# A convolution and a quick-GELU block in fast matrix forms: weight forms summed by ScalarE copies and accumulating transfers, other homes for one step's taps, and one multiply-add moved

## The chip, the core and the metric

The kernel runs on one core of one Trainium2 chip. The metric is device time in microseconds (us) of one execution. The kernel before took 2304.2 us in the median of three runs (2303.05 to 2304.34).

The engines are named as the profile names them: PE (TensorE matrix multiplies, with PEld for its weight loads), ACT (ScalarE), DVE (VectorE), POOL (GpSimd) and SP (SyncE, which here only issues transfers). Each engine works through its own queue in order; a wait at the head of a queue holds everything behind it. Transfers (DMA) are issued from the queues of SP, ACT or POOL.

## The reference

```python
# x: (8, 4096, 192) f32; weight: (8 heads, 7 taps)
w = softmax(weight)                                  # over the 7 taps
conv[b, s, d] = sum_k w[d // 24, k] * x[b, s - 6 + k, d]     # zero before the sequence
h = conv.reshape(32768, 192) @ w_in                  # w_in: (192, 2048)
g = h * sigmoid(1.702 * h)
out = g @ w_out                                      # w_out: (2048, 192)
```

## The kernel before, in words

The tokens are worked in 32 steps ("big", 0 to 31). A step takes 512 tokens of each of two halves of the batch. A step has three stages.

1. **Preparation of the step's input.** `x` is fetched by SP into `xin`, turned by DVE (`transpose_x`), and convolved into `conv_t`. The 192 channels are three blocks c = 0, 1, 2 of 64. Block 1 is summed on DVE: one multiply and six multiply-adds (`conv`, L485). Blocks 0 and 2 go by taps (`tap`): ACT multiplies the shifted input by tap k into a "home" in SBUF (L496). For block 2, POOL then adds home after home to the sum (L498). For block 0 the seven products are summed by a tree of six accumulating transfers issued from POOL's queue (L502, `TREE`), of which the fifth adds home 5 to home 3 and the sixth adds home 3 to the sum. Eight linear combinations of the sums (`sums_c`, POOL; DVE for step 1) give further inputs, and `cross` copies them to the other half of the partitions.
2. **The first product** (`hidden`, called twice per step, v = 0 and v = 1): 21 products (`TERMS`, matmuls at L584) of combined inputs with combined blocks of `w_in`, in a fast matrix form. ACT copies partial results out of PSUM (`copy2`, L621), DVE adds them (`sum2`, L625), ACT applies the GELU (L606 and L610) and writes into the tile `g`.
3. **The second product** (`second`): 25 products (matmuls at L935) of combined blocks of `g` with combined blocks of `w_out`, in an order written out by hand (`PLAN`).

While step n is in its products, step n+1 or n+2 is being prepared. The work of preparation is in two lists. `todo` holds DVE's multiply-adds of block 1 and then POOL's combinations; a call `work(us)` in `hidden` takes items from it while their planned costs (0.48 us for the first multiply, 0.76 us for a multiply-add, nothing for POOL's) fit into its budget, with 0.2 us of tolerance. `ready` holds the taps, which `next_tap` takes one by one.

The homes of the taps lie in the tile `g`, in places whose contents have been used. `spot(i)` for i of 5 and more is one block of `g`. In the steps from 3 on, block 0 uses the spots 13, 16 and 15, and block 2 the spots 14, 17 and 18 (`TAP_SPOTS`). In step 2, block 0 uses six rows of `g` of its own (`first_taps`), which share memory with spots 14, 17 and 18, where block 2 of that step has its homes. The scheduler of the program makes an instruction that overwrites a place wait for all earlier readers of it.

Step 0 is different. Its first product is plain (`plain`), its second product is `second_first`, and meanwhile the weights are rounded on DVE and combined: `w_in` by DVE (`sums_w_in`), `w_out` into the 25 "forms" by POOL (`add_forms`, L387 and L389). Fifteen forms are made at one place in `second_first`, four at its end (`SUMS_O_LATE`). Six are turned in sign later by ACT (`end_forms`, L432). The taps of step 2 are begun in `second_first`: the seven of block 0 there, the seven of block 2 in the first call of `hidden` of step 1. Step 1's `hidden` starts on PE when the last matmuls of `second_first` are done.

In one v = 0 call of `hidden` the order on DVE is: work(2.0), a sum into x, work(1.2), the two sums of k15 and k19, work(1.1), work(2.2), the sums of k20 and k16. For the steps from 2 on that is three items of block 1, then one, then three. The places in the code:

```python
sum2(vec.tensor_sub, x, z, k15)              # L680
work(1.2)                                    # L683, v = 0
sum2(vec.tensor_sub, k15, y, k19)            # L691, waits for ACT's copy k19
sum2(vec.tensor_add, k20, k20, sums)         # L709, ACT's GELU at L711 waits for it
```

Of the kernel before, what the change touches and what calls it, by code (L numbers as in the profile page):

```python
# [11 lines left out]
ALU = mybir.AluOpType  # L12
# [3 lines left out]
def kernel(  # L16
# [29 lines left out]
    nc = tc.nc  # L46

    B, S, D = x.shape
    H, K = weight.shape
# [31 lines left out]
    vec, act = nc.vector, nc.scalar  # L81
# [42 lines left out]
    def row(n, i):  # L124
        return g[:, i // NG, n, :, i % NG, :]
# [13 lines left out]
    def spot(i):  # L139

        if i >= SPOTS:
            return block(*divmod(i - SPOTS, NG))
        flat = osbs[:, i * BLK : (i + 1) * BLK] if i < 2 else room[:, ROOMS[i - 2], :]
        return flat.rearrange("p (k t) -> p k t", k=NG)

    KEPT_LATE, TAP_SPOTS = 3, {0: (13, 16, 15), 2: (14, 17, 18)}

    def kept(i):

# [26 lines left out]
    def own(big):  # L176
        return conv_t[:, big % 2 * 2, :, :]
# [41 lines left out]
    def form(i):  # L219

        if i < WHOLE:
            return w_out_s[:, i // NG, i % NG * NG : (i % NG + 1) * NG, :]
        return w_form[:, i - WHOLE, :, :]

    FORM_OF = [
        6, 4, 5, 2, 3, 0, 8, 9, 10, 11, 12, 13, 14, 15, 16, 24, 23, 17, 18, 19, 20, 7, 21, 22, 1,
    ]
    SUMS_O = [
# [3 lines left out]
    ]  # L232
    SUMS_O_LATE = [
        (23, 1, "+", 0), (24, 1, "+", 3), (1, 14, "+", 22), (7, 0, "-", 21),
    ]
    TURN_O = (9, 11, 17, 20, 7, 21)

# [71 lines left out]
    for c in range(NC):  # L309
        part = sel[:, c, :].rearrange("i (h q) -> i h q", h=2)  # L310
        for sign in (1, -1):
            nc.gpsimd.affine_select(
                out=part,
                in_=part,
# [70 lines left out]
    def add_up(v, dst, a, op, b, eng=vec):  # L385
        if op == "+":
            eng.tensor_add(v(dst), v(a), v(b))  # L387
        elif op == "-":
            eng.tensor_sub(v(dst), v(a), v(b))  # L389
        elif op == "n":  # L390
            vec.scalar_tensor_tensor(
                out=v(dst), in0=v(a), scalar=-1.0, in1=v(b), op0=ALU.mult, op1=ALU.subtract
            )
        else:
            vec.tensor_scalar_mul(v(dst), v(a), -1.0)
# [27 lines left out]
                    )  # L423
        round_piece(NW + i, dsts)

    def add_forms(items):
        for dst, a, op, b in items:
            add_up(form, dst, a, op, b, eng=nc.gpsimd)

    def end_forms():  # L430
        for i in TURN_O:
            act.mul(form(i), form(i), -1.0)  # L432
# [36 lines left out]
    taps = {c: [spot(i)[:, k : k + 2, :] for i in TAP_SPOTS[c] for k in (0, 2)] for c in TAP_SPOTS}  # L469
    first_taps = [row(0, k) for k in (6, 7, 10, 11, 14, 15)]  # L470

    def tap_home(big, c, k):
        return (first_taps if big < 3 and c == 0 else taps[c])[k - 1]

    def conv_src(big, c, k, ns=slice(0, 2)):
        return xts[big][:, c, ns, Q - PAD + k : Q - PAD + k + T]
# [15 lines left out]
    def tap(big, c, k):  # L492

        dst = own(big)[:, 2 * c : 2 * c + 2, :]
        home = tap_home(big, c, k) if k else dst
        act.mul(home, conv_src(big, c, k), cw[:, c, k : k + 1])  # L496
        if k and c not in DMA_TAPS:
            nc.gpsimd.tensor_add(dst, dst, home)  # L498
            return
        homes = [dst] + [tap_home(big, c, i) for i in range(1, K)]  # L500
        for a, b in TREE.get(k, ()):
            nc.gpsimd.dma_start(out=homes[a], in_=homes[b], accum_op=ALU.add)  # L502

    def sums_c(big, i):
        add_up(
# [87 lines left out]
    def terms(big, v, slot, *ts, first=False):  # L593
        for t in ts:
            product1(slot, *TERMS[t], big, v, first)
            first = False
# [35 lines left out]
    def hidden(big, v, x, z, y, sums, work, fetch, last=lambda: None):  # L632

        def pe(slot, *ts, first=False):
            terms(big, v, slot, *ts, first=first)

        def taps_at(n):
            for _ in range(0 if v else n):  # L640
                next_tap()

        def early(i):
            for item in EARLY_G[i] if v else ():
                sum_g(*item)


        if v:
            pe(z, 7, first=True)
            give(True, big)  # L650
        if v:
            pe(sums, 12)
            copy2(k15, sums)
            pe(x, 5, 17)
        else:
            pe(x, 5)
            pe(sums, 12)
            copy2(k15, sums)
            pe(x, 17)
            taps_at(1)  # L660
        gelu(B11, 0, v, x)
        if not v:
            pe(z, 7, first=True)
        pe(sums, 0)
        copy2(k16, sums)
        taps_at(2)
        last()
        def turn_next():
            if big + 2 < N_BIG:
                need(f"done {big + 1}")  # L670
                turn_x(big + 2)

        early(0)
        if not v:
            work(2.0 if big > 1 else 1.6)
        elif big == 1:
            work(3.2)

        pe(y, 6, 14, first=True)
        sum2(vec.tensor_sub, x, z, k15)  # L680
        early(1)
        if not v or big == 1:
            work(1.2)  # L683
        pe(sums, 13)
        copy2(k19, sums)
        pe(x, 2)
        copy2(k18, x)
        taps_at(2)
        pe(z, 11)
        pe(sums, 20, 10)  # L690
        sum2(vec.tensor_sub, k15, y, k19)  # L691
        gelu(B12, 0, v, sums)
        pe(x, 4)
        copy2(k20, x)
        sum2(vec.tensor_sub, k19, z, k19)
        early(2)
        if not v or big == 1:
            work(1.1)
        gelu(B22, 1, v, k19)
        gelu(B22, 0, v, k15)  # L700
        taps_at(2)
        pe(y, 8)
        pe(sums, 1, 9, first=True)
        pe(y, 15)
        if v and big == 1:
            turn_next()
        elif not v:
            work(2.2 if big > 1 else 1.1)
        sum2(vec.tensor_add, k20, k20, sums)  # L709
        sum2(vec.tensor_sub, k16, y, k16)  # L710
        gelu(B11, 1, v, k20)  # L711
        pe(x, 18)
        gelu(B21, 1, v, x)
        early(3)
        fetch()
        if not v:

            copy2(y, z)
        gelu(B21, 0, v, k16)
        if not v:  # L720
            work(1.2)
        if not v and big > 1:
            turn_next()
        pe(sums, 3, 19)
        if not v:
            work(0.7)
        sum2(vec.tensor_add, k18, k18, sums)
        return lambda: gelu(B12, 1, v, k18)
# [4 lines left out]
    def second_first(fetch):  # L733
# [29 lines left out]
        c11, a, c12, c21 = (slots[i][h] for h in range(2) for i in range(2))  # L763
        side = []

        def listed(w, t):
            return [(w[:, v, h, :], t[:, v, :, h * T : (h + 1) * T]) for v in range(2) for h in range(2)]
# [12 lines left out]
        def go(bank, steps, first=True, more=False):  # L780
            for i, (w, t) in enumerate(steps):
                for c in range(NC):
                    nc.tensor.matmul(
                        chunk(bank, c), w[:, chunk_cols(c)], t,
                        start=first and i == 0, stop=not more and i == len(steps) - 1, skip_group_check=True,
                    )
                if side:
                    dst, w, t, start, stop, to = side.pop(0)
                    nc.tensor.matmul(dst, w, t, start=start, stop=stop and to is not False, skip_group_check=True)
                    if to is not False:  # L790
                        act.copy(to, dst)
# [11 lines left out]
        go(a, listed(a11, b11))  # L803
        act.copy(p1, whole(a))
        go(c11, rows11[:8], more=True)
        add_forms(SUMS_O)
        work(1.5)
        sub(b12, b22, b12)  # L808
        sub(s3, a11, a21)
# [1 line left out]
        go(a, listed(s2, t2), first=False)  # L811
        act.copy(whole(c12), whole(a))
        go(c11, rows11[8:], first=False)
        work(5.0)
        add(p1, p1, whole(c11))
        turn(0, 0, blocks(p1), js)
# [2 lines left out]
        add(whole(c21), d21, whole(a))  # L819
        work(4.0)  # L820
        go(c12, listed(s4, b22) + rows12[:cut], first=False)
        fetch()
        go(c21, listed(a22, b21), first=False)
        work(3.0)
# [23 lines left out]
    def chunk(t, c):  # L848
        return t[c * Q : (c + 1) * Q]
# [143 lines left out]
    def work(us):  # L993
        while todo and todo[0][1] <= us + 0.2:
            us -= todo[0][1]
            todo.pop(0)[2]()

    def next_tap():
        if ready:
            ready.pop(0)[2]()  # L1000
            while ready and ready[0][1] == 0:
                ready.pop(0)[2]()
# [39 lines left out]
    def first_step(fetch):  # L1042
# [118 lines left out]
            fetch()  # L1161

        second_first(between)
        add_forms(SUMS_O_LATE)
        load_x(3)
        need("sums")

# [10 lines left out]
    def fetch(big, v, slot):  # L1178

        need(f"first {big}")  # L1180
        terms(big, v, slot, 16, first=True)
# [49 lines left out]
```

## Time and profile before

| what | value |
|---|---|
| median of three runs | 2304.2 us |
| the profiled execution | 2305.07 us, of which its span 2303.4 us |
| PE busy | 2279.2 us (99%) |
| DVE busy | 1963.8 us (85%) |
| ACT busy | 1551.3 us (67%) |
| POOL busy | 861.2 us (37%) |
| granted TensorE clock, mean | 0.997 |

The span is the time from the first to the last instruction of the program; the 1.7 us around it belong to the execution's time. A PE that is called busy is not always at its full rate: matmuls are pipelined, and the profile models their ends. In the timeline a row gives start, length, engine, line, operation, destination and source, count, and in brackets the idle time before it with what ended it. The chain gives start, length and what.

### The profile page before, as it was taken

What the parts mean: (1) busy time and instruction counts of PE and PEld (TensorE: products, weight loads), DVE (VectorE), ACT (ScalarE), POOL (GpSimd) and SP (SyncE); (2) the same over time, 40 slices, a digit from 0 to 9 for tenths busy, and PEclk for the clock granted to TensorE, in tenths of its full rate; (3) what the DMA queues carried; (4) which work ended last, traced back from release to release, by engine and by line L of the source; (5) the groups of instructions that cost most, each with busy time, mean ns of one, the idle gap of its engine ahead of it and who ended that gap; (6) DMA issues with size and microseconds to landing.
All of it is one profiled execution on the core that took longest, in us unless ns stands there. A gap on an engine that the chain in (4) does not pass through costs nothing.

```text
span 2303.4 us, 60981 instructions
## 1 busy us (share of the span) xinstructions
PE 2279.2 (99%) x25238; PEld 1266.0 (55%) x25238; DVE 1963.8 (85%) x2794; ACT 1551.3 (67%) x2942; POOL 861.2 (37%) x824
## 2 busy tenths in 40 slices
PE   9889999999999999999999999999999999999999
PEld 5255655655555555556655555555555555555556
DVE  8878888888888888888888888888888888888877
ACT  7267766677666776666776667776667766677654
POOL 0544433344324444234443244443344432344400
PEclk9989999999999999999999999999999999999999
DMA  8456666665665656666656666566666567564443
GB/s 186 84 109 122 116 125 138 125 125 114 122 136 121 140 115 116 125 133 129 125 114 124 136 123 138 112 115 125 137 128 127 112 122 139 121 137 87 91 97 70
DMA packets 266053, 279.82 MB, mean 121 GB/s; under 512 B 117552, under 2 KB 202928, under 8 KB 265648
## 3 DMA queue, kind: packets, MB, share of 16 engines
q0 software_dynamic: 53472, 144.73, 34.9%
q1 hardware_dynamic: 210656, 130.80, 25.3%
q8 instruction: 199, 3.26, 0.6%
q14 instruction: 78, 0.64, 0.1%
q10 hardware_dynamic: 1648, 0.39, 0.1%
HBM read 53.15 MB, written 25.17 MB: 34 GB/s over the span
## 4 chain that ended last, share of the span: by engine, by line
PE 96%; DVE 2%; DMA 1%; ACT 1%; issue 0%; SPq 0%; POOL 0%; DVEq 0%; ACTq 0%; POOLq 0%
PE slot L584 35%; PE slot L935 33%; PE sums L584 16%; PE sums L935 12%; DVE conv_t L485 1%; DMA g<-g 0%; DMA conv_t<-g 0%; DMA xin<-in_x_dram 0%; DVE g L808 0%; DVE room L800 0%; DVE xt L464 0%; DVE conv_t L389 0%; ACT g L496 0%; DVE room L799 0%; ACT conv_t L1040 0%
## 5 line engine op out<-in xcount | busy, mean ns | idle before, releaser
L584 PE MATMUL slot<-conv_t,w_in_s 64*128 64x512 f32 x3740 | 900.8, 593 | 4.0 <-ACT g L496 2.6
L935 PE MATMUL slot<-g,w_form 128*32 128x256 f32 x7024 | 710.3, 379 | 0.0
L584 PEld LDWEIGHTS slot<-conv_t,w_in_s 64*128 64x128 f32 x3740 | 426.8, 187 | 395.1 <-issue 295.9
L584 PE MATMUL sums<-conv_t,w_in_s 64*128 64x512 f32 x1660 | 444.0, 593 | 10.5 <-ACT room L621 10.2
L389 DVE TENSOR_TENSOR g<-g 128x1024 f32<-128x1024 f32 x372 | 444.3, 1222 | 4.0 <-ACT g L610 0.8
L935 PEld LDWEIGHTS slot<-g,w_form 128*32 128x32 f32 x7024 | 373.7, 110 | 119.6
L610 ACT ACTIVATE g<-room 128x1024 f32<-128x1024 f32 x310 | 324.6, 1073 | 77.4 <-DVE room L625 77.1
L960 ACT COPY room<-slot 32x256 f32<-32x256 f32 x434 | 158.9, 366 | 315.4 <-PE slot L935 313.4
L935 PE MATMUL sums<-g,w_form 128*32 128x256 f32 x2648 | 368.8, 379 | 0.0
L935 PE MATMUL slot<-g,w_out_s 128*32 128x256 f32 x4080 | 318.9, 380 | 0.0
L911 POOL DMA_DIRECT2D g<-g x124 | 106.3, 857 | 514.1 <-DVE g L389 227.8
L584 PEld LDWEIGHTS sums<-conv_t,w_in_s 64*128 64x128 f32 x1660 | 197.8, 187 | 182.7 <-issue 122.5
L498 POOL TENSOR_TENSOR conv_t<-conv_t,g 128x512 f32<-128x512 f32 x180 | 266.6, 1481 | 21.8 <-ACT g L496 5.1
L502 POOL DMA_DIRECT2D g<-g x120 | 104.3, 872 | 439.5 <-PE sums L935 128.7
L496 ACT ACTIVATE g<-xt,cw 128x512 f32<-128x512 f32 x360 | 248.6, 729 | 14.3 <-DMA conv_t<-g 12.0
L621 ACT COPY room<-slot 128x512 f32<-128x512 f32 x434 | 231.4, 601 | 34.9 <-PE slot L584 34.9
L485 DVE SCALAR_TENSOR_TENSOR conv_t<-xt,cw,conv_t 128x512 f32<-128x512 f32 (+1 forms) x210 | 231.0, 1100 | 7.9 <-ACT conv_t L483 3.1
L935 PEld LDWEIGHTS slot<-g,w_out_s 128*32 128x32 f32 x4080 | 164.7, 110 | 131.6 <-ACT g L610 13.6
L606 ACT ACTIVATE g<-slot 128x512 f32<-128x512 f32 x334 | 179.8, 592 | 47.9 <-PE slot L584 29.4
L935 PEld LDWEIGHTS sums<-g,w_form 128*32 128x32 f32 x2648 | 178.1, 110 | 36.6
L389 POOL TENSOR_TENSOR conv_t<-conv_t 128x256 f32<-128x256 f32 x180 | 184.4, 1037 | 9.4
L625 DVE TENSOR_TENSOR room<-slot,room 128x512 f32<-128x512 f32 x248 | 156.1, 680 | 37.2 <-ACT room L621 37.2
(184 smaller groups left out, 2811.4 us busy)
## 6 DMA issues: line engine op xcount, KB each, us to landing
g<-g POOLq DMA_DIRECT2D x124, 512.0 KB, 5.8
xin<-in_x_dram SPq DMA_DIRECT2D x240, 180.0 KB, 4.2
conv_t<-conv_t SPq DMA_DIRECT2D x180, 192.0 KB, 3.2
g<-g POOLq DMA_DIRECT2D x120, 256.0 KB, 3.8
out_dram<-osbs SPq DMA_DIRECT2D x186, 128.0 KB, 4.9
g<-osbs POOLq DMA_DIRECT2D x31, 512.0 KB, 4.5
g<-room POOLq DMA_DIRECT2D x31, 512.0 KB, 5.6
conv_t<-g POOLq DMA_DIRECT2D x60, 256.0 KB, 4.7
```

Source lines behind the costliest of these rows:

```text
L389: eng.tensor_sub(v(dst), v(a), v(b))
L485: vec.scalar_tensor_tensor(out=dst, in0=src, scalar=tap, in1=dst, op0=ALU.mult, op1=ALU.add)
L496: act.mul(home, conv_src(big, c, k), cw[:, c, k : k + 1])
L498: nc.gpsimd.tensor_add(dst, dst, home)
L584: nc.tensor.matmul(slot[h], w_in_s[halves[h], a, v * P : (v + 1) * P], src, start=first, stop=True, skip_group_check=True,)
L606: act.activation(dst[:, :, h, :], src[h].rearrange("p (o t) -> p o t", o=2), AF.Gelu_apprx_sigmoid)
L610: act.activation(dst.rearrange("p o h t -> p h o t"), src.rearrange("p h (o t) -> p h o t", o=2), AF.Gelu_apprx_sigmoid,)
L621: act.copy(bank(dst, h), bank(src, h))
L625: op(*(bank(t, h) for t in (dst, a, b)))
L911: nc.gpsimd.dma_start(out=spot(dst), in_=spot(a), accum_op=ALU.add)
L935: nc.tensor.matmul(dst, w, t, start=first, stop=last, skip_group_check=True)
L960: act.copy(to, d)
```

## The change

Four things change.

- `add_forms` no longer adds on POOL. For each form, ACT copies one operand into its place (or its negative, so that six later turns of sign become four), and a DMA issued from POOL's queue accumulates the other. The fifteen forms of `second_first` are spread over three places, and the four late ones stay at its end.
- In step 2, block 2's taps go to the spots 15, 16 and 19 and no longer share memory with block 0's homes.
- The tree's transfers pass through a list. In step 2 the last two are held back and issued after the late forms' transfers; in other steps they are issued where they were.
- In the steps from 2 on, the second `work` of `hidden` for v = 0 gets a budget of 1.6 in place of 1.2: two multiply-adds there, and two in place of three after the sums of k15 and k19.

The matmuls and the order of PE and SP are the same.

```diff
-    KEPT_LATE, TAP_SPOTS = 3, {0: (13, 16, 15), 2: (14, 17, 18)}
+    KEPT_LATE, TAP_SPOTS = 3, {0: (13, 16, 15), 2: (14, 17, 18), 3: (15, 16, 19)}
...
+    COPY_O = [
+        [(10, 2), (16, 1), (17, 0), (18, 0), (8, 7), (9, 5), (11, 3, -1), (12, 6, -1)],
+        [(13, 3), (14, 3), (15, 0), (19, 4), (20, 4), (21, 5), (22, 7)],
+        [],
+        [(23, 1), (24, 1), (1, 14), (7, 0, -1)],
+    ]
     SUMS_O = [
-        (8, 7, "+", 6), (9, 5, "+", 7), (10, 2, "+", 6), (11, 3, "-", 5), (12, 3, "-", 6), (13, 3, "+", 7),
-        (14, 3, "+", 2), (15, 0, "+", 2), (16, 1, "+", 5), (17, 0, "+", 10), (18, 0, "+", 16),
-        (19, 4, "+", 17), (20, 4, "+", 18), (21, 9, "+", 19), (22, 8, "+", 20),
+        [(10, 6), (16, 5), (8, 6), (9, 7), (11, 5), (12, 3)],
+        [(17, 10), (18, 16), (13, 7), (14, 2), (15, 2), (21, 7), (22, 6)],
+        [(19, 17), (20, 18), (21, 19), (22, 20)],
+        [(23, 0), (24, 3), (1, 22), (7, 21)],
     ]
-    SUMS_O_LATE = [
-        (23, 1, "+", 0), (24, 1, "+", 3), (1, 14, "+", 22), (7, 0, "-", 21),
-    ]
-    TURN_O = (9, 11, 17, 20, 7, 21)
+    TURN_O = (9, 17, 20, 21)
...
-    def add_forms(items):
-        for dst, a, op, b in items:
-            add_up(form, dst, a, op, b, eng=nc.gpsimd)
+    def add_forms(stage):
+        for dst, src, *sign in COPY_O[stage]:
+            if sign:
+                act.mul(form(dst), form(src), -1.0)
+            else:
+                act.copy(form(dst), form(src))
+        for dst, src in SUMS_O[stage]:
+            nc.gpsimd.dma_start(out=form(dst), in_=form(src), accum_op=ALU.add)
...
     def tap_home(big, c, k):
-        return (first_taps if big < 3 and c == 0 else taps[c])[k - 1]
+        if big < 3:
+            return (first_taps if c == 0 else taps[3])[k - 1]
+        return taps[c][k - 1]
...
         for a, b in TREE.get(k, ()):
-            nc.gpsimd.dma_start(out=homes[a], in_=homes[b], accum_op=ALU.add)
+            tree.append((homes[a], homes[b]))
+        end_taps(2 if big < 3 and k == K - 1 else 0)
+
+    tree = []
+
+    def end_taps(left=0):
+        while len(tree) > left:
+            out, src = tree.pop(0)
+            nc.gpsimd.dma_start(out=out, in_=src, accum_op=ALU.add)
...
         if not v or big == 1:
-            work(1.2)
+            work(1.6 if big > 1 else 1.2)
...
         go(c11, rows11[:8], more=True)
-        add_forms(SUMS_O)
+        add_forms(0)
...
         go(c11, rows11[8:], first=False)
+        add_forms(1)
         work(5.0)
...
         go(c12, listed(s4, b22) + rows12[:cut], first=False)
+        add_forms(2)
         fetch()
...
         second_first(between)
-        add_forms(SUMS_O_LATE)
+        add_forms(3)
+        end_taps()
         load_x(3)
```

## The prediction

> **What bounds the kernel now.** I read the page's busy shares and its chain first: PE carries the end nearly everywhere, so only time that PE loses can be won or added.
>
> ```profile
> PE 2279.2 (99%) x25238; PEld 1266.0 (55%) x25238; DVE 1963.8 (85%) x2794; ACT 1551.3 (67%) x2942; POOL 861.2 (37%) x824
> PE 96%; DVE 2%; DMA 1%; ACT 1%; issue 0%; SPq 0%; POOL 0%; DVEq 0%; ACTq 0%; POOLq 0%
> ```
>
> Next, PE's own waits. Apart from some at the start they all lie before step 1 ends:
>
> ```profile
> PE sums L584 <- ACT room L621: 10.2, 1, 10.2
> PE slot L584 <- ACT g L496: 2.6, 1, 2.6
> PE slot L783 <- DVE slot L819: 1.1, 1, 1.1
> PE slot L584 <- DVE conv_t L840: 0.7, 1, 0.7
> PE slot L783 <- issue: 0.6, 1, 0.6
> ```
>
> Then the chain, for the pace of the steps. The second product starts at 153.48 in step 1 and at 2264.10 in step 31 (the first and the last), and the rows between are one undisturbed step: 36.25 us from the first L584 to the first L935, and 70.06 us from one second product to the next.
>
> ```profile
> 153.48 3.80 PE slot L935 x67
> 1420.12 3.80 PE slot L935 x67
> 1453.93 4.49 PE slot L584 x20
> 1490.18 0.98 PE slot L935 x13
> 2264.10 3.80 PE slot L935 x67
> ```
>
> Thirty steps of 70.06 would be 2101.8; the last one prepares nothing and lacks one of its terms, four matmuls of 4.49/20 us, which leaves 2100.9. It took 2264.10 - 153.48 = 2110.6. So 9.7 us are lost in the steady steps, in pieces too short to show as idle time of PE.
>
> Last, the timeline around step 1, PE first, then ACT and POOL:
>
> ```profile
> 100.57 1.22 PE L584 MATMUL slot<-conv_t,w_in_s 64*128 64x512 f32 x4 [2.58 <-ACT g L496]
> 104.95 0.69 PE L584 MATMUL slot<-conv_t,w_in_s 64*128 64x512 f32 x1 [0.71 <-DVE conv_t L840]
> 121.46 4.27 PE L584 MATMUL sums<-conv_t,w_in_s 64*128 64x512 f32 x8 [10.23 <-ACT room L621]
> 127.86 2.12 PE L584 MATMUL sums<-conv_t,w_in_s 64*128 64x512 f32 x8
> 138.14 1.18 PE L584 MATMUL slot<-conv_t,w_in_s 64*128 64x512 f32 x3 [0.43 <-ACT room L621]
> ...
> 107.45 0.73 ACT L496 ACTIVATE g<-xt,cw 128x512 f32<-128x512 f32 x1
> 120.22 0.72 ACT L496 ACTIVATE g<-xt,cw 128x512 f32<-128x512 f32 x1 [12.04 <-DMA conv_t<-g]
> 120.84 1.05 ACT L621 COPY room<-sums 128x512 f32<-128x512 f32 x2
> ...
> 113.69 1.20 POOL L502 DMA_DIRECT2D conv_t<-g  x1 [5.18 <-DMA g<-g]
> 118.83 1.26 POOL L498 TENSOR_TENSOR conv_t<-conv_t,g 128x512 f32<-128x512 f32 x1
> ```
>
> The reader sees one story. Block 2's second tap of step 2 wants to overwrite a place that the tree's last transfer (issued at 113.69) still reads. ACT stands for 12.04 us; queued behind that tap are the copies that free `sums`, and PE stands for 10.23. Step 1's first product takes 153.48 - 100.57 = 52.9 us, 16.7 more than the undisturbed 36.25.
>
> **The parts of those 16.7 us.** 10.23 is the wait. After it PE runs slowly: 16 matmuls start between 121.46 and 127.86, 6.40 us, where the undisturbed pace (4.49/20 each) needs 3.6: 2.8 lost. The granted clock says why:
>
> ```profile
> 121.46:138.00 16.54, 16.25 (x60) 12.97 (x60) 12.08 (x14) 14.75 (x27) 10.65 (x10) 0.82 0.04 8
> ```
>
> The columns are length, PE, PEld, DVE, ACT, POOL, then PEclk 0.82. The rest, 16.7 - 10.2 - 2.8 = 3.7, is the wait on L840, the one at 138.14, and half steps beside them. The Trainium skill (TensorE: Matmul & The Clock Gate, "What's actually happening") has the array fall to half rate after an idle window and return after about 3.4 us of busy time; by that the slow restart would cost some 1.7 us as an estimate, and the sum below would be 1.1 smaller. The row is the larger and I use it.
>
> **Change 1: step 2's homes.** The tap at 120.22 loses its conflict: spots 15, 16 and 19 are the other half of `g`, last read by `second_first`, whose matmuls are over before any of these taps. So ACT goes on at about 108.2 (107.45 + 0.73), the copies of 120.84 run eleven microseconds earlier, and PE neither waits nor cools: 10.2 + 2.8 = 13.0. Late next: POOL's adds for block 2, still queued behind the tree, and the ACT queue's own length (below).
>
> **Change 2: forms by copies and DMAs.** What goes: POOL's nineteen adds, of which the first fifteen run from 59.01 to 84.2. They slow DVE, which carries the chain there:
>
> ```profile
> 59.01 7.28 POOL L387 TENSOR_TENSOR w_form<-w_out_s 128x384 f32<-128x384 f32 x3 [54.92 <-DVE w_out_s L372]
> 81.31 2.87 POOL L387 TENSOR_TENSOR w_form<-w_form 128x384 f32<-128x384 f32 x2
> ...
> 61.23 2.91 DVE L800 TENSOR_TENSOR room<-g,room 128x2048 f32<-128x2048 f32 x1
> 75.02 4.32 DVE L485 SCALAR_TENSOR_TENSOR conv_t<-xt,cw,conv_t 128x512 f32<-128x512 f32 x3
> 84.58 2.24 DVE L817 TENSOR_TENSOR g<-g,room 128x2048 f32<-128x2048 f32 x1
> 87.35 3.10 DVE L485 SCALAR_TENSOR_TENSOR conv_t<-xt,cw,conv_t 128x512 f32<-128x512 f32 x4
> 93.09 2.09 DVE L464 STREAM_TRANSPOSE xt<-xin 128x576 f32<-128x576 f32 x3
> ...
> 62.88 0.58 ACT L791 COPY room<-sums 32x512 f32<-32x512 f32 x1 [2.89 <-PE sums L789]
> 71.11 0.56 ACT L812 COPY slot<-slot 96x512 f32<-96x512 f32 x1
> 135.03 1.76 ACT L432 ACTIVATE w_form<-w_form 128x384 f32<-128x384 f32 x4
> ```
>
> A multiply-add costs 1.44 beside POOL (75.02) and 0.78 after it (87.35), the large sum 2.91 against 2.24. Seven multiply-adds (0.66 each) and two large sums (0.67 each) make 6 us; for four small sums beside POOL I add 2, an estimate. A little is given back where DVE waits for others, so the transposes at 93.09 come about 7 earlier. With them go the waits on DVE: 0.6 ("issue", where L802 had just ended), 1.1 (L819), and most of the 2.6 before step 1, where ACT's taps started only after these transposes. By the rows 4.3; I take 4.3, with 4.9 as the upper end, because idle time is counted from the modelled end of a matmul and PE starts are a little further apart.
>
> L840's 0.7 in step 1 goes too: the DVE queue ahead of it is 7 us less late.
>
> What is added on ACT: 19 copies at 1.76/4 = 0.44 us, less two turns of sign: 7.5 us net. Fifteen go in two lots behind the rows at 62.88 and 71.11, where ACT mostly waits for PE (2.89 ahead of the first). Behind them stand the copies out of `sums` of `second_first` and one multiply for DVE (some 3 us late); PE reuses those banks only about 7 us later, and DVE's next consumer on PE's path is L819, about 6 us early by then. Cost 0; without that cover up to 3. The four late ones (1.8 us) stand right before step 1's first copies, with ACT's taps just done: PE needs `sums` again after four terms. I charge 1.2 for them, as some idle time of ACT takes the rest.
>
> What is added on POOL: 21 transfers, up to 1.2 us of queue each (row at 113.69), in place of 19 adds. The price of one transfer of 196 KB is not shown; the nearest is the tree's 256 KB:
>
> ```profile
> g<-g POOLq DMA_DIRECT2D x4, 256.0 KB, 5.4
> ```
>
> Pipelined from about 64 on, at a microsecond of queue each, the first seventeen are landed at about 87, ahead of the tree. One after another they would take 17 x 5.4 = 92 us; that end is a rival. The four late ones and the held-back pair: block 0's last tap is done at about 97, home 5 has its sum one landing later, home 3 a second one later, and POOL's block 2 adds start at about 109 in place of 118.83, some 13 us into step 1 instead of the 9 usual in later steps; the first value made from them is needed at the end of that step's first product, about 7 us after it is there.
>
> **Change 3: the multiply-add.** One slow and one undisturbed step:
>
> ```profile
> 333.00 0.74 DVE L485 SCALAR_TENSOR_TENSOR conv_t<-xt,cw,conv_t 128x512 f32<-128x512 f32 x1
> 335.35 1.29 DVE L625 TENSOR_TENSOR room<-sums,room 128x512 f32<-128x512 f32 x2 [1.61 <-ACT room L621]
> 337.75 5.10 DVE L485 SCALAR_TENSOR_TENSOR conv_t<-xt,cw,conv_t 128x512 f32<-128x512 f32 x3
> 344.08 1.06 ACT L610 ACTIVATE g<-room 128x1024 f32<-128x1024 f32 x1 [0.75 <-DVE room L625]
> ...
> 1464.04 4.12 DVE L485 SCALAR_TENSOR_TENSOR conv_t<-xt,cw,conv_t 128x512 f32<-128x512 f32 x3
> 1469.50 1.07 ACT L610 ACTIVATE g<-room 128x1024 f32<-128x1024 f32 x1
> ```
>
> Three multiply-adds stand ahead of the sum k20. Beside POOL's block 2 adds they take 4.12 to 5.10 us, and where they take 5.10, ACT's GELU of k20 waits 0.75, and behind it in ACT's queue are the GELU and the copies that free the banks PE needs next. After the change one of the three runs right behind the row at 333.00, where DVE then idles for 1.61 us and POOL is not yet adding: 0.74 fits. The group shrinks to two, 3.4 (two thirds of 5.10), below the harmless 4.12. So the 9.7 us should go; I take 9.5. POOL's combinations lose nothing: the last multiply-add comes earlier.
>
> **Sum.** Start 4.3; step 1: 16.7 less a remainder. The remainder lies between 0 and 3.7 + 1.8 = 5.5; I take 1.5 (the 1.2 above and 0.3 of the wait at 138.14, behind which only four turns of sign stand instead of six), so 15.2. Steady steps 9.5. Together 29.0. The profiled execution took 2305.07 us (2303.4 span, 1.7 around it): 2276.1. The median of the runs is 0.9 below it: **2275.2 us**.
>
> **Rivals.**
> - The steady steps keep their loss, because the stall moves to another wait of the same ACT queue, which has no idle time to spare there: without the 9.5, 2284.7. Against it: in undisturbed steps ACT has the same queue and PE loses nothing. 9 in 100.
> - Step 1 finds a new wait of a few microseconds, from POOL's later adds or ACT's longer queue, and PE cools again: remainder 9 instead of 1.5, 2282.7. For it: POOL starts its adds 4 us later in the step than usual, and DVE is slow beside them. 13 in 100.
> - The accumulating transfers go one after another. ACT's last form copies wait for the twelfth to land. With the first issued at about 64 and 5.4 each, it lands at 129 and ACT, which is there at 97, stands 32 us with PE behind it: the total gain of 29 becomes a loss of 3 to 6, 2308 to 2311. It decides from 5 us for each transfer on. Against it: most of the first seventeen build on no other form, so POOL need not wait between them. 3 in 100. The Trainium skill (SBUF — State Buffer, "Who interferes with whom") warns that DVE can keep GpSimd from writing the descriptors of its transfers; no row here shows such a stretch.
> - The moved multiply-add runs beside POOL and takes 1.7 (5.10/3): it passes the 1.61 by 0.1, 29 times: 3 us less gain, 2278, within my own case.
>
> **How the numbers follow.** My case has 72 in 100 and the range 2271.9 to 2280: all bounds at their best give 4.9 + 16.7 + 9.7 = 31.3, that is 2272.9, less one for the spread of the runs; the upper end has the remainder at 5.5. The two rivals with part of the gain reach to 2285, so the range is 2271.9 to 2286. Measurement tells 0.2% from no change, 4.6 us here. Faster by more than that: 94 in 100; within it: 2; slower: 4.
>
> **What the new profile would show.** No wait of ACT on a transfer near 110, no idle of PE over 1 us in step 1, granted clock 1.0 there; multiply-adds near 0.75 us between 65 and 83; step 1's first product starting near 96 and its second near 134; and all thirty steps at 70.06. Wrong would be: a step that still takes 70.7, ACT standing at the late form copies, or PE waiting in step 1 for POOL's combinations.

## The result

The changed kernel took 2283.9 us (median of four runs, 2282.6 to 2286.1) beside 2303.6 for the kernel before: a ratio of 0.9918, interval 0.9900 to 0.9935, a gain of 19.7 us. The forecast was 2275.2 in a range of 2271.9 to 2286.0: the direction is right and the time lies inside the range, but near its upper end, 8.7 us from the predicted value. The likeliest case did not happen. What happened is the second rival, a new wait in step 1.

The profiled execution took 2282.62 us (span 2280.6), 22.45 less than the profiled one of before (2305.07). Its page, busy shares and chain:

```profile
PE 2267.5 (99%) x25238; PEld 1196.6 (52%) x25238; DVE 1930.9 (85%) x2794; ACT 1558.3 (68%) x2959; POOL 839.4 (37%) x826
PE 96%; DVE 1%; DMA 1%; POOL 1%; ACT 1%; issue 0%; SPq 0%; DVEq 0%; POOLq 0%; ACTq 0%
```

PE still carries the end. PE's waits in steps 1 and later (waited for: us in total, times, longest):

```profile
PE slot L956 <- DVE g L393: 5.0, 1, 5.0
PE slot L603 <- DVE room L644: 0.3, 1, 0.3
PE sums L603 <- ACT room L640: 0.2, 1, 0.2
```

The 10.2, 2.6, 1.1, 0.7 and 0.6 of before are gone. One wait of 5.0 is new. The timeline of PE places it, and the chain gives the pace of the steps; the chain's rows shown are the start of step 2 and that of step 30:

```profile
95.64 1.13 PE L603 MATMUL slot<-conv_t,w_in_s 64*128 64x512 f32 x4
134.04 0.42 PE L956 MATMUL slot<-g,w_out_s 128*32 128x256 f32 x3
146.19 0.65 PE L956 MATMUL slot<-g,w_out_s 128*32 128x256 f32 x3 [5.04 <-DVE g L393]
```

```profile
174.54 4.49 PE slot L603 x20
2136.17 4.49 PE slot L603 x20
```

Step 1 starts at 95.64 instead of 100.57, which is 4.93 gained. Its first product takes 38.40 us (95.64 to 134.04) instead of 52.9, 14.5 gained. The steps from 2 on take (2136.17 - 174.54)/28 = 70.06 each, so the 9.7 of the steady steps are gained whole. But step 1's second product, with the new wait in it, takes 40.4 us instead of 33.81 (70.06 - 36.25), 6.6 lost. 4.9 + 14.5 + 9.7 - 6.6 = 22.5, the whole difference. Without the 6.6 the profiled time would have been 2276.0, against the 2276.1 of the forecast's sum. That it agrees to a tenth is luck: the start brought 0.6 more than its term, step 1's first product 0.7 less, the steady steps 0.2 more, and these misses cancel.

**Where the 6.6 come from.** DVE's and POOL's timelines of the changed kernel, the latter from the tree's third transfer to the one that DVE waits for:

```profile
142.65 4.75 DVE L393 TENSOR_TENSOR g<-g 128x1024 f32<-128x1024 f32 x4 [6.21 <-DMA g<-osbs]
```

```profile
97.42 1.19 POOL L521 DMA_DIRECT2D g<-g  x1 [2.26 <-ACT g L507]
99.40 2.27 POOL L437 DMA_DIRECT2D w_form<-w_out_s  x2
100.50 2.94 POOL L437 DMA_DIRECT2D w_out_s<-w_form  x2
101.98 2.68 POOL L521 DMA_DIRECT2D g<-g  x1
114.92 1.19 POOL L521 DMA_DIRECT2D conv_t<-g  x1 [10.26 <-DMA g<-g]
115.68 11.09 POOL L509 TENSOR_TENSOR conv_t<-conv_t,g 128x512 f32<-128x512 f32 x6
...
130.81 3.90 POOL L393 TENSOR_TENSOR conv_t<-conv_t 128x256 f32<-128x256 f32 x4
134.66 0.88 POOL L932 DMA_DIRECT2D g<-osbs  x1
```

Read it backwards. PE waits at 146.19 for a combination that DVE makes in `g` (L393). DVE has stood 6.21 us for the accumulating transfer `g<-osbs` (L932, which adds spot 0 to spot 8; it is one of the sums of blocks of `g` that `hidden` makes ahead of the second product, listed in `EARLY_G`). POOL issues that transfer only at 134.66, after the second product has begun, because six adds and eight combinations of block 2 stand ahead of it, and these began at 115.68. They began late because the head of POOL's queue was the tree's sixth transfer, which stood 10.26 us for the fifth. The fifth (101.98) was queued behind the four late forms. The chain gives the two landings:

```profile
101.98 12.66 DMA g<-g
134.66 7.96 DMA g<-osbs
```

The fifth took 12.66 us to land, where the forecast had 5.4. After its wait PE also runs slowly; the window right behind it, of the changed kernel (length, then busy time of PE, PEld, DVE, ACT and POOL, then the granted clock, DMA share and GB/s):

```profile
146.20:150.00 3.80, 3.80 (x48) 1.86 (x52) 3.80 (x5) 0.37 (x1) 0.86 (x1) 0.63 0.56 157
```

A clock of 0.63 for 3.8 us is 1.4 us lost; with the 5.04 of the wait that makes 6.4 of the 6.6.

### The profile page after: what moved, and what is told of

It reads as the page before. It is cut to its first block, busy times and chain, and to the rows that moved or that the text cites. A ratio compares the mean times of both kernels' runs of the same rounds, so it can differ in the third digit from the quotient of the medians.

```text
span 2280.6 us, 60969 instructions
## 1 busy us (share of the span) xinstructions
PE 2267.5 (99%) x25238; PEld 1196.6 (52%) x25238; DVE 1930.9 (85%) x2794; ACT 1558.3 (68%) x2959; POOL 839.4 (37%) x826
## 4 chain that ended last, share of the span: by engine, by line
PE 96%; DVE 1%; DMA 1%; POOL 1%; ACT 1%; issue 0%; SPq 0%; DVEq 0%; POOLq 0%; ACTq 0%
PE slot L603 34%; PE slot L956 33%; PE sums L603 15%; PE sums L956 12%; PE slot L802 1%; DMA g<-g 1%; POOL conv_t L509 0%; DMA g<-osbs 0%; DVE conv_t L496 0%; POOL conv_t L393 0%; DVE xt L473 0%; DMA xin<-in_x_dram 0%; DVE w_in_s L391 0%; DVE osbs L874 0%; ACT w_form L435 0%
## 5 line engine op out<-in xcount | busy, mean ns | idle before, releaser
L603 PE MATMUL slot<-conv_t,w_in_s 64*128 64x512 f32 x3740 | 861.1, 591 | 0.6 <-DVE room L644 0.3
L603 PEld LDWEIGHTS slot<-conv_t,w_in_s 64*128 64x128 f32 x3740 | 371.4, 187 | 430.3 <-issue 355.0
L393 DVE TENSOR_TENSOR g<-g 128x1024 f32<-128x1024 f32 x372 | 450.1, 1237 | 9.6 <-DMA g<-osbs 6.2
L603 PE MATMUL sums<-conv_t,w_in_s 64*128 64x512 f32 x1660 | 407.4, 589 | 0.5 <-DVE w_in_s L376 0.3
L932 POOL DMA_DIRECT2D g<-g x124 | 106.3, 857 | 494.7 <-PE sums L956 153.9
L603 PEld LDWEIGHTS sums<-conv_t,w_in_s 64*128 64x128 f32 x1660 | 170.2, 187 | 188.1 <-issue 141.9
L509 POOL TENSOR_TENSOR conv_t<-conv_t,g 128x512 f32<-128x512 f32 x180 | 261.4, 1452 | 15.2 <-POOL conv_t L509 3.9
L640 ACT COPY room<-slot 128x512 f32<-128x512 f32 x434 | 231.7, 602 | 38.7 <-PE slot L603 38.7
L496 DVE SCALAR_TENSOR_TENSOR conv_t<-xt,cw,conv_t 128x512 f32<-128x512 f32 (+1 forms) x210 | 194.0, 924 | 10.6 <-ACT conv_t L494 5.9
L393 POOL TENSOR_TENSOR conv_t<-conv_t 128x256 f32<-128x256 f32 x180 | 181.9, 1025 | 9.4
L981 ACT COPY room<-sums 32x256 f32<-32x256 f32 x217 | 79.6, 367 | 144.3 <-PE sums L956 142.6
```

The source lines that it names most:

```text
L496: vec.scalar_tensor_tensor(out=dst, in0=src, scalar=tap, in1=dst, op0=ALU.mult, op1=ALU.add)
L603: nc.tensor.matmul(slot[h], w_in_s[halves[h], a, v * P : (v + 1) * P], src, start=first, stop=True, skip_group_check=True,)
L640: act.copy(bank(dst, h), bank(src, h))
L932: nc.gpsimd.dma_start(out=spot(dst), in_=spot(a), accum_op=ALU.add)
L981: act.copy(to, d)
```

## The experiments

**Each part alone.** Three kernels that differ from the one before by one part each.

Change 1, step 2's homes:

```diff
-    KEPT_LATE, TAP_SPOTS = 3, {0: (13, 16, 15), 2: (14, 17, 18)}
+    KEPT_LATE, TAP_SPOTS = 3, {0: (13, 16, 15), 2: (14, 17, 18), 3: (15, 16, 19)}
...
     def tap_home(big, c, k):
-        return (first_taps if big < 3 and c == 0 else taps[c])[k - 1]
+        if big < 3:
+            return (first_taps if c == 0 else taps[3])[k - 1]
+        return taps[c][k - 1]
```

> The kernel before with change 1 alone (other homes for step 2's taps). My theory: ACT no longer stands for 12 us, PE neither waits 10.2 nor runs 2.8 slow, so 13.0 less if nothing else is late. But POOL's adds for block 2 start no earlier than in the kernel before (about 119), its combinations end at about 141, and the accumulating transfer behind them lands about 146 while the second product of step 1 now starts near 140.5: I expect PE to wait there some 2 to 3 us and to run slow after it, so 9 to 11 us less, about 2293. Rival (the wait is simply gone, nothing takes its place): 2290.6 or less.

Measured: 2290.5 us (2289.3 to 2290.9), ratio 0.9946 (0.9930 to 0.9963), 12.9 less than the kernel before, run beside it (2303.4). That is the rival (2290.6 or less), and my theory was wrong in a detail that matters: I had the new wait come with the homes alone, and it does not. In this kernel's timelines of POOL and DVE the accumulating transfer goes out even later than in the changed kernel, yet DVE hardly waits:

```profile
118.77 10.20 POOL L500 TENSOR_TENSOR conv_t<-conv_t,g 128x512 f32<-128x512 f32 x6
136.75 0.87 POOL L913 DMA_DIRECT2D g<-osbs  x1
```

```profile
142.67 4.75 DVE L389 TENSOR_TENSOR g<-g 128x1024 f32<-128x1024 f32 x4 [0.81 <-DMA g<-osbs]
```

The second product starts at 139.7 here, and PE loses nothing in it. So it is not how late POOL is that counts, but how late against PE. The prediction's 13.0 for the conflict with the tree stands at 12.9; the interval of the ratio means a gain of 8.5 to 16.1 us, so the agreement to a tenth says little, and what carries the point is that ACT's and PE's waits of 12.0 and 10.2 are gone from the trace.

Change 2, the forms by copies and accumulating transfers, with the two last transfers of the tree held back behind the late forms as in the diff (homes and multiply-add as before):

> The kernel before with change 2 alone (forms by copies and accumulating transfers, the last two of the tree behind the late forms; old homes, old multiply-add). My theory: step 1 starts 4.9 us earlier, as in the changed kernel, but block 2's second tap still waits for the tree's last transfer, which in the changed kernel lands at 120.2 instead of 120.1: ACT stands about 17 us instead of 12, and PE loses what the start won, so 2302 to 2306, no change. Rival (the forms alone carry the start-up's gain): about 2299 or less.

Measured: 2303.6 us (ten runs, 2299.8 to 2305.5), ratio 1.0001 (0.9992 to 1.0010). Nothing, as expected, though step 1 starts at 95.6, 5 us earlier. ACT's and PE's timelines of this kernel show where the gain goes:

```profile
120.21 0.72 ACT L505 ACTIVATE g<-xt,cw 128x512 f32<-128x512 f32 x1 [17.09 <-DMA conv_t<-g]
```

```profile
121.46 4.27 PE L601 MATMUL sums<-conv_t,w_in_s 64*128 64x512 f32 x8 [16.05 <-ACT room L638]
```

PE is sooner at the same stand and leaves it at the same 121.46 as before: 16.05 us of wait where there were 10.23. With the conflict of the homes in place, an earlier start is worth nothing.

Change 3, the multiply-add:

```diff
-            work(1.2)
+            work(1.6 if big > 1 else 1.2)
```

> The kernel before with change 3 alone (the multiply-add moved). My theory: all steady steps at 70.06 us, 9.6 us less, about 2294. Rival (the steady steps' loss hangs on when the taps and POOL start, which the start-up sets): less than 6 us of gain, some steps still at 70.7.

Measured: 2294.3 us (2293.6 to 2295.4), ratio 0.9963 (0.9948 to 0.9977), 9.1 less, and every step from 2 on takes 70.06. To see whether this one number is really the lever, I turned it the other way:

```diff
-            work(1.2)
+            work(0.4 if big > 1 else 1.2)
```

> The kernel before with the lever of change 3 pulled the other way: no multiply-add at the second place, four in the group ahead of the sum of k20. My theory (the length of that group beyond 4.4 us is what PE loses, step by step): the group takes 5.6 to 6.9 us, each steady step loses 1.2 to 2.5 us instead of 0.33, so 25 to 60 us slower than before, 2330 to 2365, and ACT's GELU of k20 waits for DVE in every step. Rival (the loss comes from the taps and POOL and not from the group): within 5 us of before.

Measured: 2347.4 us (2346.2 and 2348.5), ratio 1.0188 (1.0168 to 1.0209), 43.5 more. DVE's and ACT's timelines, and ACT's wait over the whole run:

```profile
340.88 6.86 DVE L485 SCALAR_TENSOR_TENSOR conv_t<-xt,cw,conv_t 128x512 f32<-128x512 f32 x4
```

```profile
348.97 1.06 ACT L610 ACTIVATE g<-room 128x1024 f32<-128x1024 f32 x1 [2.51 <-DVE room L625]
```

```profile
ACT g L610 <- DVE room L625: 122.1, 93, 2.5
```

The same wait in the kernel before:

```profile
ACT g L610 <- DVE room L625: 77.1, 82, 1.2
```

The group of four shown takes 6.86 us beside POOL and ACT's GELU waits 2.51 behind it; the groups of three in the kernel before took 4.1 to 5.2, with a wait of up to 0.9. Most of these waits are harmless ones elsewhere in the step: with change 3 alone 65.9 us in 63 waits are left, while every step from 2 on takes 70.06. The rest, which comes and goes with the group, is some 11 us before (77.1 - 65.9) and 56 here (122.1 - 65.9). The dose and the loss go together, by the mechanism that the prediction gave.

**The parts together.** Changes 1 and 3 without change 2:

> Changes 1 and 3 without change 2: the forms are still added on POOL. If the two add up: 2303.4 - 12.9 - 9.1 = 2281.4, faster than the changed kernel by 2 to 3 us, which says that change 2 in the order in which it issues its transfers costs more than it brings. Rival (change 2 brings its 4.9 us at the start as predicted and the loss in the second product belongs to changes 1 and 3): 2287 or more.

Measured: 2282.2 us (2281.9 to 2282.7), ratio 0.9905 (0.9891 to 0.9920) against 2303.9. The two parts add up: 2303.4 - 12.9 - 9.1 = 2281.4. This kernel starts step 1 at 100.45 and yet takes no longer than the changed one, so change 2, as it stands, brings about nothing on top of the other two: its 4.9 at the start is paid back by the 6.6. (The 2 to 3 us that I expected it to cost did not come out clearly; see the repeats below.)

**Is it the place in the queue?** The changed kernel with the tree's fifth transfer issued ahead of the late forms, the sixth behind them. The work is the same:

```diff
         second_first(between)
+        end_taps(1)
         add_forms(3)
         end_taps()
```

> The changed kernel, but of the two held-back transfers of the tree the fifth is issued ahead of the four late forms, the sixth still behind them. Theory of the queue: in the changed kernel the fifth landed at 114.6, 12.7 us after its issue, behind the four late forms; with it ahead it lands near 107, POOL's adds start near 108 instead of 115.7, the accumulating transfer into g goes out near 127 instead of 134.7, and PE's wait of 5.0 us in the second product of step 1 goes with the slow restart behind it: 6 to 6.6 us less than the changed kernel, about 2277. Rival (the adds on POOL are slow beside DVE, or the accumulating transfer lands late for the traffic of x): the wait stays at 3 us or more, 2281 or more.

Measured: 2275.2 us (2275.22 to 2275.32), ratio 0.9879 (0.9865 to 0.9894), 28.2 less than the kernel before. POOL's and DVE's timelines:

```profile
101.96 1.19 POOL L521 DMA_DIRECT2D g<-g  x1 [2.19 <-DVE slot L644]
108.78 1.20 POOL L521 DMA_DIRECT2D conv_t<-g  x1 [2.04 <-DMA g<-g]
109.52 10.06 POOL L509 TENSOR_TENSOR conv_t<-conv_t,g 128x512 f32<-128x512 f32 x6
128.32 0.88 POOL L932 DMA_DIRECT2D g<-osbs  x1
```

```profile
134.12 5.89 DVE L393 TENSOR_TENSOR g<-g 128x1024 f32<-128x1024 f32 x5
```

PE's timeline, the start of step 1 and of its second product:

```profile
95.58 1.13 PE L603 MATMUL slot<-conv_t,w_in_s 64*128 64x512 f32 x4
133.29 0.42 PE L956 MATMUL slot<-g,w_out_s 128*32 128x256 f32 x3
```

The fifth is issued at the same moment as in the changed kernel (101.96 against 101.98), with nothing else of that batch ahead of it, and lands at 108.2 instead of 114.6. POOL's adds start at 109.52 (the forecast had 109), the accumulating transfer goes out 5 us ahead of the second product (133.29), DVE does not wait, and neither does PE: the second product takes 33.81. The first product takes 37.71 where the changed kernel took 38.40, so 0.7 of that one's loss belonged to POOL's lateness too. 6.6 and 0.7 make 7.3 of the 7.4 us between the two profiled executions (2282.62 and 2275.24). By the medians one line moved is worth 8.7 us here and 5.0 in the repeats below.

**Is it that transfer that PE waits for?** The changed kernel with the order left as it is, but in step 1 the sum of spots 0 and 8 made by DVE itself instead of by the transfer:

```diff
             for item in EARLY_G[i] if v else ():
+                if big == 1 and item[2] == "acc":
+                    item = (8, 8, "+", 0)
                 sum_g(*item)
```

> The changed kernel, but in step 1 the sum of spot 0 into spot 8 is made by DVE and not by an accumulating transfer behind POOL's adds. Theory of the queue: that transfer is the only thing PE waits for in step 1's second product, so the wait of 5.0 us and the slow restart go as they did with the fifth transfer ahead, at the price of one 1.2 us addition on DVE; about 2276 to 2278. Rival (another late result stands right behind it, the values of POOL's combinations or the next accumulating transfer): a wait of 2 us or more stays, 2280 or more.

Measured: 2276.5 us (2276.1 to 2277.1), ratio 0.9880 (0.9864 to 0.9897). The wait of 5.0 is gone though POOL is as late as before, so it was this transfer that brought it. It is not the only way by which POOL's lateness reaches PE. Near the end of step 1's first product PE waits for POOL's first combinations, which `cross` copies (`conv_t<-conv_t`); PE's timeline of this kernel:

```profile
131.20 3.59 PE L603 MATMUL slot<-conv_t,w_in_s 64*128 64x512 f32 x12 [0.50 <-DMA conv_t<-conv_t]
```

With that wait and the slower stretch behind it the first product takes 39.21 us here (95.51 to 134.72), 1.5 more than with the fifth transfer ahead, and that is nearly the whole difference of the two profiled executions (2276.81 and 2275.24). The rival was right in kind, then, and wrong in size. In the changed kernel PE stops at the same place for 0.3 us (the wait at L603 shown in the result); the profile puts that one down to a sum of DVE which ended at about the same time.

**The spread.** The changed kernel's runs lie further apart than those of its relatives, so it was run again beside two of them:

> The changed kernel once more, beside the next one on the same chip. In its first four runs it took 2282.6 to 2286.1 us, a spread of 3.5 where the kernel with the fifth transfer ahead had 0.1. If the spread belongs to the wait for the accumulating transfer in step 1, it comes back here, around 2284, and the profile shows a wait of 4 to 8 us there.

> Changes 1 and 3 without change 2 once more, in the same call as the changed kernel, to settle the sign of change 2: 2281.5 to 2282.5, so 1 to 2.5 us faster than the changed kernel. Rival: no difference beyond 0.5 us.

> The changed kernel with the tree's fifth transfer ahead of the late forms, once more: 2275 to 2276, 8 to 9 us faster than the changed kernel and 28 faster than before.

Measured: the changed kernel 2280.2 us (2278.28, 2278.38, 2282.07, 2285.60), ratio 0.9905 (0.9890 to 0.9920); changes 1 and 3 without 2, 2282.5 (2282.4 to 2283.2), 0.9911 (0.9897 to 0.9926); the fifth ahead 2275.2 (2275.15 to 2275.38), 0.9880 (0.9863 to 0.9896). The times of the last two came as expected; that of the changed kernel did not. It was not near 2284 but 3.7 us lower. So it lies 5.0 above the kernel with the fifth ahead and not 8 to 9, and it was 2.2 us faster than changes 1 and 3 without 2, where I had expected it to be slower. Its profiled execution, again its fastest, has the same wait, smaller. PE's wait, DVE's and POOL's timelines, and a window that begins shortly before the wait ends:

```profile
PE slot L956 <- DVE g L393: 2.4, 1, 2.4
```

```profile
139.70 4.75 DVE L393 TENSOR_TENSOR g<-g 128x1024 f32<-128x1024 f32 x4 [3.43 <-DMA g<-osbs]
```

```profile
113.89 1.19 POOL L521 DMA_DIRECT2D conv_t<-g  x1 [9.27 <-DMA g<-g]
132.64 0.88 POOL L932 DMA_DIRECT2D g<-osbs  x1
```

```profile
142.40:146.20 3.80, 2.95 (x56) 1.84 (x60) 3.77 (x4) 0.37 (x1) 0.32 (x1) 1.00 1.05 255
```

The transfer goes out 2 us earlier and landed in 7.0 instead of 8.0 us. PE waits 2.4 instead of 5.0 and its clock stays at 1.00. I had expected a wait of 4 to 8 us. Four profiled executions fit one condition: the second product starts at 139.7, 133.3, 133.6 and 134.0 (homes alone, fifth ahead, and the changed kernel's two), DVE has the transfer 2.9, 0.9, 6.1 and 8.6 us after that, and PE waits 0, 0, 2.4 and 5.0. Changes 1 and 3 together (3.1 and 2.8 us) and the second execution of the fifth ahead (2.5) fit too, without a wait. What comes later than about 3.6 us after the start of the second product is lost. In the changed kernel that hangs on when several queued transfers land. With the fifth ahead there is slack, and eight runs lie within 0.25 us. That the changed kernel's other runs, which have no trace, differ by the same wait is inferred from this and not shown; their mean granted clocks, 1.000, 1.000, 0.999 and 0.998 in the order of the four times above, fit it. Nor is it settled whether change 2 as it stands brings a little or costs a little: 2283.9 against 2282.2 by the first medians, 2280.2 against 2282.5 by the second.

## Why the prediction was right, and where it was wrong

- **Step 1's wait, 13.0: right.** 12.9 alone, within a wide interval. In the changed kernel ACT goes from tap to tap near 110 without a wait on a transfer, and PE's granted clock is 1.00 from 96 to 134. One aside of the prediction does not follow: a cheaper slow restart would not take 1.1 off its sum, because the sum takes the whole 16.7 less a remainder, and how those 16.7 divide into wait and restart does not enter it.
- **The start, 4.3 (to 4.9): right, at its upper end.** Step 1 starts 4.93 earlier. DVE's timeline of the changed kernel has the multiply-adds without POOL beside them, 2.32/3 = 0.77 each instead of 1.44, and the transposes 7.3 us earlier, where "about 7" was forecast:

```profile
69.06 2.32 DVE L496 SCALAR_TENSOR_TENSOR conv_t<-xt,cw,conv_t 128x512 f32<-128x512 f32 x3
85.82 2.09 DVE L473 STREAM_TRANSPOSE xt<-xin 128x576 f32<-128x576 f32 x3
```

- **The copies on ACT: right that they are hidden.** The four late ones left PE 0.2 us of wait for ACT (L640). The first product takes 2.15 over its undisturbed 36.25; the remainder charged was 1.5. With the fifth transfer ahead it takes 1.46 over, so what is left of the 2.15 is POOL's lateness and not the copies.
- **The transfers pipeline: right for fifteen of the first seventeen.** Issued from 64 to 77, those fifteen have landed at 84.3, mostly 1.0 to 1.3 us apart. The last two build on other forms, and POOL stood 6.02 us for a landing before it could issue them, so they landed at 89.4 and 92.0 (87 in the forecast). That cost nothing here: between 60 and 95 PE does not wait. DMA issues of the changed kernel between 55 and 92 (KB each, median us to landing), and POOL's stand:

```profile
w_form<-w_out_s POOLq DMA_DIRECT2D x11, 192.0 KB, 6.1
w_form<-w_form POOLq DMA_DIRECT2D x6, 192.0 KB, 7.3
```

```profile
83.86 0.86 POOL L437 DMA_DIRECT2D w_form<-w_form  x1 [6.02 <-DMA w_form<-w_form]
```

  By these medians they take longer to land than the tree's 5.4, but they overlap, so the rival of 2308 to 2311 did not come.
- **The steady steps, 9.5: right.** 9.1 by the change alone, 9.7 in the trace. Groups of two multiply-adds, one ahead of POOL's adds and one beside them, from the DVE timeline of the changed kernel, and ACT's GELU behind them, which no longer waits:

```profile
320.02 1.53 DVE L496 SCALAR_TENSOR_TENSOR conv_t<-xt,cw,conv_t 128x512 f32<-128x512 f32 x2
324.77 2.65 DVE L496 SCALAR_TENSOR_TENSOR conv_t<-xt,cw,conv_t 128x512 f32<-128x512 f32 x2
```

```profile
330.23 1.07 ACT L629 ACTIVATE g<-room 128x1024 f32<-128x1024 f32 x1
```

  The group ahead runs at 0.77 each, clear of POOL, so the rival in which it runs beside POOL fell as well.
- **The four late forms and the held-back pair: wrong, and with it the remainder of step 1.** Two things failed in that step. First, a size: the fifth transfer was given one landing time, 5.4 us, as if it were alone, but four transfers of 192 KB stood ahead of it on the same queue; it took 12.66, and POOL's adds started at 115.7 instead of 109. The seventeen transfers had been added up as a stream in that same prediction; the four were not. Second, a consumer was left out: "the first value made from them is needed at the end of that step's first product, about 7 us after it is there" looks at what is made from POOL's adds, and not at what is queued behind them, the accumulating transfer that the second product needs about 3.6 us after its start. Before the change PE was late enough for it (second product at 153.48, and still at 139.7 with the homes alone). With both changes PE came to 134.0, and POOL was no longer early. The consumer that the prediction did name, PE in the first product, cost 0.7. Of its signs of being wrong, "PE waiting in step 1 for POOL's combinations" came in this small form, and "no idle of PE over 1 us in step 1" failed by the wait of 5.0.
- **The rival with a new wait after which PE cools again, 2282.7, is what came** (2282.62 in the profiled execution), by "POOL's later adds" as it said and not by ACT's queue. It had 13 in 100. Its condition was not the one it gave: it had POOL start its adds 4 us later in the step than usual, at 109, and with the fifth transfer ahead they start at 109.5 without a wait; it took a start at 115.7. Its price was not worked out to the consumer behind the adds either, so that 2282.7 and 2282.62 agree is luck, and the four runs beside it lie at up to 2286.1. The range held because it reached to this rival.

With the fifth transfer ahead of the late forms, all the steps of the forecast come true at once: the start brings 5.0, the first product its 15.2, the steady steps 9.7, and PE does not wait in the second product. The time is 2275.2, the forecast's value; to the tenth that is luck, since these parts add up to 0.9 more than the forecast's 29.0, and the forecast had taken off 0.9 for the median of the runs. That is the better version of this kernel: 28.2 us less than before and, by the medians, 8.7 and 5.0 less than the change as made.

## What to carry to other kernels

A transfer's time to landing is read with the queue ahead of it: when several go out in one batch, the one whose landing blocks the issuing engine goes first. When two gains bring the bounding engine forward, every engine that fed it in time must be looked at again against the new start, to the end of its queue and not only to the first value that it makes. Gains of separate parts add up only where no such consumer lies between: here 12.9 and 9.1 did, and the third part was worth about nothing as made and 7 us (2282.5 to 2275.2) with one line in another place.

## What the runs showed of the hardware

- The same accumulating transfer of 256 KB, issued within 0.2 us of 102, took 12.7 and 11.5 us to landing behind four others of 192 KB (the changed kernel's two profiled executions; 12.1 and 12.7 in the two other kernels with that order) and 6.3 and 7.6 ahead of them (the reordered one's): 3.9 to 6.4 more, 1.0 to 1.6 us for each transfer in front. The earlier ones landed mostly 1.0 to 1.3 us apart, one behind the other, which fits. The fetch of x, which shares the DMA engines at that time, begins at 101.4 and 101.3 in the first execution of either order, so its start does not make the difference; what it adds to both was not varied.
- A wait of PE of 2.42 us left the granted clock at 1.00, one of 5.04 was followed by 0.63 over 3.8 us. The Trainium skill (TensorE: Matmul & The Clock Gate, "What's actually happening") puts the fall of the clock at an idle window of about 3.4 us or more; these two waits lie on either side of it and agree. The 2.8 us lost after the 10.23 of the kernel before (a granted clock of 0.55 over the 6.40 us from 121.46) are more than the 1.7 that one such window at half rate would cost by that section as an estimate; after 5.04 the trace has 1.4.
- DVE's operations with two inputs in SBUF cost more beside POOL's adds: a multiply-add 1.44 against 0.77, the large sum 2.91 against 2.29. The Trainium skill (SBUF — State Buffer, "Who interferes with whom") says that such an instruction contends with a GpSimd one that reads SBUF; the rows agree, and moving the adds from POOL into transfers freed DVE as that section would have it.
